# Stage four of a Fourier mixing kernel in quarters of the matmul array, from batch 3

## The chip, the core and the metric

The kernel runs on one core of a Trainium2 chip. The metric is the device time of one execution in microseconds (us). A core has five engines that run side by side and wait for each other by semaphores: TensorE (PE, matrix products), VectorE (DVE), ScalarE (ACT), GpSimd (POOL) and SyncE (SP, which here issues most DMA transfers). Products are written to PSUM, which has eight banks; a bank holds 128 partitions of 512 fp32 numbers.

## What is computed

```python
X = np.fft.rfft(x, axis=1)                    # x: (8, 2496, 256)
Y = X * (filt_r + 1j * filt_i)[None, :, :]
y = np.fft.irfft(Y, n=2496, axis=1).reshape(8 * 2496, 256)
logits = y @ w_gate                           # (19968, 8)
expert = argmax(logits, axis=1)               # gate = its softmax share
for e in range(8):                            # rows sorted by expert
    out[rows of e] = relu(y[rows of e] @ w1[e]) @ w2[e]   # 256 -> 1024 -> 256
out *= gate[:, None]
```

## The kernel before

**The transform.** 2496 = 39 x 64, and the 2496-point transform is done as transforms of 39 and 64 points. For each of the 8 batches there are four stages, each a product with a constant table on PE:

- Stage one (`stage_a`, table `tas`): 39 real points to 20 complex coefficients. Three of the 64 residues stand beside each other on the partitions (3 x 39 = 117 rows in, 3 x 40 = 120 rows out), and 22 *columns* of 256 numbers follow each other. A *chunk* is four columns, the last chunk of a batch two: `CH`. The result goes to DRAM (`zd`).
- Stage two (`stage_b`, `tbs`): 64 points, then DVE multiplies by the filter. Stage three (`stage_c`, `tcs`): 64 points back; the result goes to DRAM (`ud`), one DMA for each four frequencies.
- Stage four (`stage_d`, `tds`): 20 complex coefficients back to 39 real points. A chunk is loaded from `ud` (`load_u`), one product of 512 output columns (120 rows deep, 128 wide) makes two columns of y, and DVE or ACT copies it from its bank into `yo`. The 22nd column holds one residue instead of three, so the last chunk of a batch takes two products of 256, 120 and 40 rows deep.

**Gate and routing.** From `yo` come the logits: for batches 3 to 7 (`by_blocks`) DVE transposes in blocks of 32, and `block_logits` multiplies by the gate weights in four strips of 32 columns of the array. `route` finds the expert and the place of each row, and POOL writes id and gate (eight copies each) behind each row of `yo`, and scatters one column at a time, 117 rows, into the expert's part of `rowsd` (`scatter`), 22 scatters per batch.

**Experts.** As rows of an expert come together, tiles of 512 or 256 rows are read back (`rows_in`), multiplied by w1 and w2 (in part by a scheme with seven block products for eight), scaled by the gate and scattered to the output.

**The order.** All instructions are written in an order that the kernel plans while it is built. The class `Order` keeps an estimated time for each engine and counts a price for each instruction. The main loop, at the end, offers the steps of the transform of slot k (stages two and three of batch k, stage one of batch k+1, stage four of batch k-1) and the two streams of expert products, and takes the first that is ready by the estimate. Each engine then runs its own list strictly in that order. Every call goes through the recording layer, so that the profile shows line 246 for all of them; groups are told apart by the names of their tiles. DMA loads and stores are issued on SP, each in its turn.

Of the kernel before, what the change touches and what calls it, by code (L numbers as in the profile page):

```python
# [34 lines left out]
TK = NB * NS  # L35
DH = D // P
# [4 lines left out]
NJ = D // CT  # L41

# [13 lines left out]
def dft_tables():  # L56
# [24 lines left out]

    ids = np.zeros((NB, N1, NG))
    valid = np.zeros((NB, N1, NG))
    for j in range(NB):
# [3 lines left out]

    by_block = np.zeros((4, CT, NG + 2))
    by_block.reshape(P, NG + 2)[:TP, :NG] = valid.reshape(TP, NG)  # L90
# [5 lines left out]
        "ta": ta.reshape(TP, TK),  # L96
        "tb": tb,
        "tc": tc,
        "td": np.pad(td.reshape(TK, TP), ((0, 0), (0, P - TP))),
        "sg": np.concatenate([sg[:, :NF // 2], sg[:, NF // 2:]]),  # L100
        "ids": ids.reshape(TP, NG),
        "valid": np.concatenate([np.pad(valid.reshape(TP, NG), ((0, P - TP), (0, 0))), by_block], axis=1),
    }


def lay_x(x):

    out = np.zeros((x.shape[0], P, NG, D), x.dtype)
    q = np.arange(N1)
    for j in range(NB):  # L110
        for i in range(len(range(j, N2, NB))):
            out[:, j * N1:(j + 1) * N1, i] = x[:, token(q, NB * i + j)]
    return out
# [11 lines left out]
class Order:  # L125
# [53 lines left out]
    def count(self, engine, op, args, named):  # L179
# [31 lines left out]
        else:  # L211
            if out is None:
                took = 0.8 if engine == "sync" else 0.02
            elif engine == "tensor":
                if start > self.busy + 1.2:
                    self.slow = start + 3.4
                rows = out.ap[0][1]
                took = max(0.1, 0.00085 * n) if op == "transpose" else max(0.216, 0.00169 * n) if rows > 32 else 0.00045 * n
                took *= 2.0 if start < self.slow else 1.0
                tail = 0.25  # L220
            elif engine == "vector":
                took = 0.15 + n / 960
            elif engine == "scalar":
                took = 0.16 + n / 1200
            else:
                took = 0.2 + n / 480
# [24 lines left out]
class Slots:  # L251
# [3 lines left out]
    def freed(self, name, tag):  # L255

        if name is None:
            return 0.0
        if tag in self.live and name in self.live[tag]():
            return 1e9  # L260
        return max(self.order.done.get(name, 0.0), self.order.used.get(name, 0.0)) + 0.1
# [32 lines left out]
def kernel(  # L294
# [12 lines left out]
    ids: bass.AP,  # L307
    valid: bass.AP,
# [25 lines left out]
    TR = E * TE  # L334

    dram = open_pool(ctx, name="dram", bufs=1, space=DRAM)
    zd = [dram.tile([N2, NS, D], F32, tag=f"z{b % 2}", name="zd") for b in range(B)]
    ud = [dram.tile([N2, NS, D], F32, tag=f"u{b % 2}", name="ud") for b in range(B)]


    DR = D + 16
    rowsd = dram.tile([TR, DR], F32, tag="rows", name="rows")
# [17 lines left out]
    tas = cst.tile([TP, TK], F32, name="tas")  # L360
    tbs = cst.tile([P, P], F32, name="tbs")
    tcs = cst.tile([P, P], F32, name="tcs")
    tds = cst.tile([TK, P], F32, name="tds")
# [15 lines left out]
    ids0 = cst.tile([TP, NG], F32, name="ids0")  # L379
    vld = cst.tile([P, 2 * NG + 2], F32, name="vld")  # L380
# [12 lines left out]
    ps.live["bank"] = lambda: ()  # L393
# [25 lines left out]
    def load_filters(c):  # L419
        f0, n = FH[c]  # L420
        if c == 0:
            nc.sync.dma_start(out=tbs, in_=tb)
# [11 lines left out]
        if c == 0:  # L434
            nc.sync.dma_start(out=tcs, in_=tcm)

    def load_rest():
        nc.sync.dma_start(out=tds, in_=td)
# [33 lines left out]
    def columns(ap, i0, n):  # L472

        rows = ap.rearrange("t s d -> (t s) d")
        m = min(n, NG - 1 - i0)
        yield TK, slice(0, m), rows[i0 * TK:(i0 + m) * TK, :].rearrange("(i p) d -> p i d", p=TK)
        if m < n:
            yield NS, slice(m, n), rows[(NG - 1) * TK:, :].rearrange("(i p) d -> p i d", p=NS)
# [23 lines left out]
    def by_part(ap):  # L502

        return ap.rearrange("t (c f) d -> (t c) f d", c=2)

# [8 lines left out]
    def load_z(b, c):  # L514
        f0, n = FH[c]
        zi = fin(("z", b, c))
        nc.sync.dma_start(out=zi[:, :n], in_=by_part(zd[b])[:, f0:f0 + n, :])

    def load_u(b, c):
        i0, n = CH[c]  # L520
        ui = fin(("u", b, c))
        for r, m, v in columns(ud[b], i0, n):
# [5 lines left out]

    def stage_a(b, c):
        i0, n = CH[c]  # L530
        xt = ins.pop(("x", b, c))
        zo = sb.tile([TK, 4, D], F32, tag="st", name="zo", bufs=4)
        for j in range(0, n, 2):
            p = bank()
            mm(p[:TK, :], lhsT=tas, rhs=xt[:TP, j:j + 2, :], start=True, stop=True)
            evac(zo[:, j:j + 2, :], p[:TK, :].rearrange("p (t d) -> p t d", t=2), 512)
        for r, m, v in columns(zd[b], i0, n):
# [4 lines left out]
    def stage_b(b, f):  # L542
# [6 lines left out]
        mm(p, lhsT=tbs, rhs=zi[:, j:j + 2, :], start=True, stop=True)  # L549
# [13 lines left out]

    def stage_c(b, f):
# [6 lines left out]
        mm(p, lhsT=tcs, rhs=ys, start=True, stop=True)  # L571
        evac(uo[:, j:j + 2, :], p.rearrange("p (i d) -> p i d", i=2), 512)
        if j == 2:
            f0 = f - 2
            move(by_part(ud[b])[:, f0:f0 + 4, :], uo)
# [3 lines left out]
    def stage_d(b, c):  # L579
# [7 lines left out]
        yo = outs["o", b, c] = sb.tile([P, 4, DR], F32, tag="y", name="yo", bufs=YB)  # L587
        for j in range(0, n, 2):
            p = bank()
            if i0 + j + 2 < NG:  # L590
                mm(p, lhsT=tds, rhs=ui[:TK, j:j + 2, :], start=True, stop=True)
# [6 lines left out]


# [12 lines left out]
    def first_a(c):  # L612
        i0, n = CH[c]
        xt = ins.pop(("x", 0, c))
        for j in range(0, n, 2):
            p = bank()[:, :4 * TK]
            for h in range(DH):
                for i in range(2):
                    mm(p[:, (2 * h + i) * TK:(2 * h + i + 1) * TK], lhsT=xt[:TP, j + i, h * P:(h + 1) * P], rhs=tas,
# [21 lines left out]
    def first_c(f):  # L641
        ys = outs.pop(("y", 0, f))
        p = bank().rearrange("p (h i t c) -> p h i t c", h=DH, c=2, i=2)
        for i in range(2):
            for h in range(DH):
                mm(p[:, h, i].rearrange("p t c -> p (t c)"), lhsT=ys[:, i, h * P:(h + 1) * P],
                   rhs=tcs, start=True, stop=True)
# [90 lines left out]
    def route(b, c0, c1):  # L738
# [63 lines left out]
        if by_blocks(b):  # L802
# [13 lines left out]
            nc.vector.tensor_copy(row.rearrange("p (c g) -> p g c", g=4), pr[:, :, 0])  # L816
# [5 lines left out]
        for i, yo in enumerate(yos):  # L822
            n = min(4, w - 4 * i)
            sh8 = (TP, n, 8)
            nc.gpsimd.tensor_scalar(
                yo.bitcast(I32)[:TP, :n, D:D + 8], in0=ids0[:, t0 + 4 * i:t0 + 4 * i + n, None].to_broadcast(sh8),
# [3 lines left out]
        for i in range(w):  # L830
            m = N1 if t0 + i == NG - 1 else TP
            rows.append((row[:m, i:i + 1], yos[i // 4][:m, i % 4, :]))
        for i, (at, what) in enumerate(rows):
            m = what.ap[0][1]
            nc.gpsimd.tensor_copy(what[:, D + 8:], sd[:m, i:i + 1].to_broadcast((m, 8)))
# [7 lines left out]
    def pad_rows():  # L843
# [7 lines left out]
        nc.gpsimd.memset(fill.bitcast(I32)[:, D:D + 8], N)  # L851
# [96 lines left out]
    def rows_in(i):  # L948
# [4 lines left out]
        ng = gis[i] = pools["moe"].tile([P, 4, DR - D], F32, tag="ng", name="ng", bufs=8)  # L953
# [128 lines left out]
    def result(i, j):  # L1082
# [12 lines left out]
        gate = gis[i][:, j, 8:9]  # L1095
# [49 lines left out]
    def result_by_quarters(i):  # L1145
# [7 lines left out]
        gate = gis[i][:, :, 8:9]  # L1153
# [62 lines left out]
    def slot(k):  # L1216
# [12 lines left out]
        elif k < B:  # L1229
            for f in range(0, NF + 4, 2):  # L1230
                at = f / (NF + 4)
                if f < NF:
                    steps.append((at, lambda f=f: stage_b(k, f), ("z", k, f // 4) if f % 4 == 0 else None, 0.85, "b", lambda f=f: count("y") < 4 and [ins["z", k, f // 4]]))
                if f >= 4:
                    steps.append((at + 0.01, lambda f=f: stage_c(k, f - 4), None, 0.85, "c", lambda f=f: [outs["y", k, f - 4], 0.0 if f % 4 else sb.free("st") - 0.9]))
        if k + 1 < B:
            for c in range(nch):
                steps.append(((0.25 if k == 0 else 0.0) + 0.7 * c / nch, lambda c=c: stage_a(k + 1, c), ("x", k + 1, c), 0.43 * CH[c][1], "a", lambda c=c: [ins["x", k + 1, c], sb.free("st") - 0.9]))
        if k > 0:
            for c in range(nch + 3):  # L1240
# [3 lines left out]
                if c < nch:  # L1244
                    steps.append((at, lambda c=c: stage_d(k - 1, c), ("u", k - 1, c) if k > 1 else "y", 0.43 * CH[c][1], "d",
                                  lambda c=c: [ins["u", k - 1, c] if k > 1 else outs["ui", c], sb.free("y") - 0.9]))
                if by_blocks(k - 1):
                    if 1 <= c <= nch:
                        steps.append((at + 0.03, lambda c=c: turn_y(k - 1, c - 1), None, 0.0, "d", lambda c=c: len(yts) < 2 and [outs["o", k - 1, c - 1]]))
# [174 lines left out]
    def second_products():  # L1424

        for i in range(NT - RARE):
            if late and i < LARGE:
# [37 lines left out]
    with tc.manual_schedule(engines=None):  # L1465
        warm()
        nc.sync.dma_start(out=tas, in_=ta)
# [5 lines left out]
        def wait_of(f):  # L1473
# [11 lines left out]
            banks = ps.free("bank") if f[3] < 0.9 else max(ps.free("bank"), ps.free("bank", 1) - 0.85)  # L1485
# [15 lines left out]
        while fs or any(heads):  # L1501
# [7 lines left out]
            choice[0 if credit > 0.0 or not fs else 1:0] = products  # L1509
# [64 lines left out]
```

## Time and profile before

| | |
|---|---|
| median of 3 runs | 1470.89 us (1468.29 to 1471.23) |
| the profiled execution | 1474.5 us, its span 1472.8 us |
| mean granted PE clock | 0.992 |
| PE products of stage four, 512 columns, from DRAM | x140 records, 606 ns mean, 67.4 us busy |
| row scatters on POOL | x176, 1034 ns mean |
| result scatters on POOL (128 rows) | x161, 1003 ns mean |
| y copies, ACT and DVE | x82 of 588 ns, x6 of 681 ns |
| DMA | 278.19 MB, mean 189 GB/s |

A group of the profile is written as line, engine, operation, output tile <- input tiles, shapes, count, then busy time in us and the mean in ns. The records of PE overlap: a record's length covers also the time that its data takes through the array, so the pace is read from the starts. One fp32 product stands as two MATMUL records. The shape `120*128` in a PE row is rows times columns of the array in use. "PEld" are weight loads. In the page's 40 slices PE has 8 or 9 tenths in nearly all of them, and DMA is above 8 tenths in most of the first nine.

### The profile page before, as it was taken

Reading aid. Unit: us, or ns where it says so; the run is one execution under the profiler, and the core shown is the slowest. Engines: PE = TensorE matmul, PEld = TensorE weight load, DVE = VectorE, ACT = ScalarE, POOL = GpSimd, SP = SyncE. Lnnn points to the kernel's source line nnn. Section 1 sums busy time; section 2 is a strip of 40 time slices with the busy share of each in tenths; the row PEclk is TensorE's granted clock in tenths of the full one; section 3 lists DMA queues with packets and bytes.
Section 4 is the critical chain, followed back from the end, with each engine's and each line's share of the span. In section 5 each row is a group of like instructions: output and inputs, shape, how many; then the busy total and the mean of one; then the engine's idle time right before and its main releaser. Section 6 shows DMA issues by size and latency. Waiting matters only on the chain.

```text
span 1472.8 us, 25703 instructions
## 1 busy us (share of the span) xinstructions
PE 1438.4 (98%) x7828; PEld 1148.5 (78%) x7828; DVE 835.8 (57%) x1818; ACT 480.5 (33%) x1005; POOL 818.9 (56%) x1214
## 2 busy tenths in 40 slices
PE   8998999999999999999999999999999999999998
PEld 5553555777577777777787778889999999999997
DVE  4666568335766574566757554566878775531110
ACT  3553443233232333222223232222232322223332
POOL 3434355525456654565375567647989878831111
PEclk9999999999999999999999999999999999999999
DMA  9749798887786576557345644548665424456661
GB/s 255 243 156 339 250 323 257 271 260 222 246 246 189 169 253 180 150 167 251 105 126 151 205 117 132 149 128 244 175 186 154 133 77 139 135 191 176 173 192 42
DMA packets 216383, 278.19 MB, mean 189 GB/s; under 512 B 124131, under 2 KB 163708, under 8 KB 216245
## 3 DMA queue, kind: packets, MB, share of 16 engines
q1 hardware_dynamic: 197125, 233.19, 53.7%
q0 software_dynamic: 19120, 43.33, 8.5%
q8 instruction: 66, 1.08, 0.3%
q14 instruction: 72, 0.59, 0.1%
HBM read 196.45 MB, written 80.64 MB: 188 GB/s over the span
## 4 chain that ended last, share of the span: by engine, by line
PE 85%; DMA 6%; DVE 4%; issue 2%; POOL 1%; SPq 1%; ACT 1%; POOLq 0%; DVEq 0%; ACTq 0%
PE bank L246 85%; DMA fin<-in_x_dram 2%; DMA fin<-ud 2%; DVE yw L246 1%; DVE ys L246 1%; DMA ud<-uo 1%; DMA fin<-zd 1%; SPq L246 1%; POOL out_dram L246 0%; DVE hT L246 0%; DMA w1t<-in_moe_w_dram 0%; DMA ng<-rows 0%; ACT hT L246 0%; DMA zd<-zo 0%; DMA xg<-rows 0%
## 5 line engine op out<-in xcount | busy, mean ns | idle before, releaser
L246 DVE TENSOR_TENSOR hT<-bank,hT 128x512 f32<-128x512 f32 (+1 forms) x504 | 300.8, 626 | 165.4 <-PE bank L246 77.7
L246 PE MATMUL bank<-w2t,hT 128*128 128x256 f32 (+1 forms) x1984 | 387.5, 350 | 2.4 <-DVE hT L246 1.4
L246 PEld LDWEIGHTS bank<-w2t,hT 128*128 128x128 f32 x1984 | 335.1, 190 | 53.0 <-issue 11.7
L246 PE MATMUL bank<-xT,w1t 128*128 128x256 f32 (+1 forms) x1728 | 316.3, 329 | 0.2 <-DVE hT L246 0.2
L246 POOL DMA_INDIRECT out_dram<-ys,ng x161 | 161.5, 1003 | 271.6 <-ACT ys L246 136.7
L246 PEld LDWEIGHTS bank<-xT,w1t 128*128 128x128 f32 x1728 | 265.4, 192 | 32.4 <-issue 8.3
L246 ACT ACTIVATE hT<-hT 128x1024 f32<-128x1024 f32 (+1 forms) x144 | 135.0, 959 | 390.5 <-DVE hT L246 387.5
L246 POOL DMA_INDIRECT rows<-yo,row x176 | 181.9, 1034 | 74.8 <-POOL yo L246 38.5
L246 ACT ACTIVATE ys<-bank,ng 128x256 f32<-128x256 f32 x104 | 49.3, 474 | 303.9 <-PE bank L246 235.2
L246 PE MATMUL bank<-sums,wsum 128*128 128x256 f32 (+1 forms) x576 | 135.6, 358 | 0.0
L246 PE MATMUL bank<-w2s,hT 128*128 x592 | 132.6, 379 | 0.0
L246 PEld LDWEIGHTS bank<-w2s,hT 128*128 128x128 f32 x592 | 110.3, 190 | 13.8
L246 PEld LDWEIGHTS bank<-sums,wsum 128*128 128x128 f32 x576 | 100.5, 190 | 17.7 <-issue 6.8
L246 POOL TENSOR_TENSOR wsum<-w1t 128x256 f32<-128x256 f32 x72 | 56.5, 785 | 82.2 <-PE bank L246 57.7
L246 DVE STREAM_TRANSPOSE xT<-xg 128x512 f32<-128x512 f32 (+2 forms) x126 | 57.4, 493 | 54.6 <-PE bank L246 51.4
L246 DVE TENSOR_TENSOR ys<-bank,ht 128x512 f32<-128x512 f32 x80 | 54.8, 685 | 52.2 <-PE bank L246 42.9
L246 PE MATMUL bank<-fin,tas 117*120 117x512 f32 x154 | 77.3, 622 | 6.9 <-DMA fin<-in_x_dram 6.7
L246 PE MATMUL bank<-fin,tds 120*128 120x512 f32 (+1 forms) x168 | 76.1, 573 | 3.9 <-DMA fin<-ud 3.3
L246 PE MATMUL bank<-fin,tbs 128*128 128x512 f32 x140 | 72.6, 605 | 5.4 <-DMA fin<-zd 5.4
L246 PE MATMUL bank<-ys,tcs 128*128 128x512 f32 x140 | 73.3, 611 | 4.2 <-DVE yw L246 3.4
L246 ACT ACTIVATE hT<-bank 128x128 f32<-128x128 f32 (+1 forms) x191 | 57.6, 303 | 52.5 <-PE bank L246 42.9
L246 PE MATMUL bank<-xT,wsum 128*128 128x256 f32 (+1 forms) x288 | 67.8, 358 | 0.2 <-ACT yo L246 0.2
(171 smaller groups left out, 1766.6 us busy)
## 6 DMA issues: line engine op xcount, KB each, us to landing
w1t<-in_moe_w_dram SPq DMA_DIRECT2D x126, 512.0 KB
w2t<-in_moe_w_dram SPq DMA_DIRECT2D x68, 512.0 KB
fin<-in_x_dram SPq DMA_DIRECT2D x39, 512.0 KB
fin<-zd SPq DMA_DIRECT2D x35, 512.0 KB
ud<-uo SPq DMA_DIRECT2D x35, 512.0 KB
fin<-ud SPq DMA_DIRECT2D x35, 512.0 KB
zd<-zo SPq DMA_DIRECT2D x35, 480.0 KB
xg<-rows SPq DMA_DIRECT2D x112, 128.0 KB
```

What stands on the lines that cost most here:

```text
L246: return real(*args, **named)
```

## The change

It has these parts:

1. **Quarters.** From batch 3 (`BD = 3`) the rows of a column are laid out so that the 60 real parts lie on partitions 0 to 59 and the 60 imaginary ones on 64 to 123; partitions 60 to 63 and 124 to 127 are pads. A chunk's four products each use 60 rows and 64 columns of the array, with 512 output columns (256 in a last chunk): one product for each pair of (real or imaginary rows) and (first or second half of the chunk's columns). Real rows give the even half of the 39 points, imaginary rows the odd half, each in a bank of its own. The odd half is copied to `yo`, then `fold_y` makes even + odd and even - odd by two DVE instructions that read the even half in its bank.
2. **Tiles of u apart.** Batches 3 to 7 write u into two DRAM tensors of their own (`halves_apart`). A store of stage three becomes two, of 126 and of 2 partitions (`by_part`). `fill_between` writes the pads and the last column once, with filter values, in slot 1: four DMAs.
3. **Row scatters of 128 rows.** The rows of a column in the new layout fill all 128 partitions. Rows that stand for no token get places behind the experts' parts (320 for each batch, `lids`), chosen by a maximum when the row numbers are made. `DR` falls from 272 to 264: id and gate are written four times instead of eight.
4. **Tables** are loaded into [128, 128] tiles, each a second time later on (`load_table`). The same layout is written for stages one and two from batch `BA = 8`, which no batch reaches.
5. **The planner** gets prices for products of 64 rows out, a rule for the bank that a fold still needs, changed rules for free banks and for the order of choices, and one rule for the start of the last expert products. The tile for ids and gates (`ng`) has 7 buffers instead of 8.

```diff
+BA, BD = 8, 3
...
+                if op == "matmul" and rows == 64 and n > D // 2:
+                    took = 0.29 if n > D else 0.17
...
-    ud = [dram.tile([N2, NS, D], F32, tag=f"u{b % 2}", name="ud") for b in range(B)]
+    ud = [dram.tile([NG * P, D], F32, tag=f"u{b % 2}", name="ud") for b in range(BD)]
+    halves_apart = [dram.tile([NG * P, D], F32, tag=f"v{b}", name="ud") for b in range(2)]
+    ud[BD:] = [halves_apart[b % 2] for b in range(B - BD)]
...
-    DR = D + 16
-    rowsd = dram.tile([TR, DR], F32, tag="rows", name="rows")
+    DR = D + 8
+    rowsd = dram.tile([TR + NW * B, DR], F32, tag="rows", name="rows")
...
-    ps.live["bank"] = lambda: ()
+    ps.live["bank"] = lambda: {p.name for key, p in outs.items() if key[0] == "odd"}
...
+    def fill_between():
+        for u in halves_apart:
+            at = u[TH, :]
+            nc.sync.dma_start(out=bass.AP(at.tensor, at.offset, [[64 * D, 2 * NG - 2], [1, 4 * D]]), in_=ht[:2 * NG - 2, :4, :].rearrange("p f d -> p (f d)"))
+            nc.sync.dma_start(out=u[(NG - 1) * P:, :], in_=ht[:, 0, :])
...
-            move(by_part(ud[b])[:, f0:f0 + 4, :], uo)
+            for of, v in by_part(ud[b], uo, b >= BD, f0, 4):
+                move(v, of)
...
+        if b >= BD:
+            m = n // 2
+            both = [bank() for _ in range(2)]
+            for h in range(2):
+                for part in range(2):
+                    k = slice(64 * part, 64 * part + TH)
+                    mm(both[part][64 * h:64 * h + 64, :m * D].rearrange("p (i d) -> p i d", i=m), lhsT=tds[k, :64],
+                       rhs=ui[k, h * m:(h + 1) * m, :], start=True, stop=True)
+            evac(yo[:, m:n, :D], both[1][:, :m * D].rearrange("p (i d) -> p i d", i=m), m * D)
+            outs["odd", b, c] = both[0]
+            return
...
+    def fold_y(b, c):
+        m = CH[c][1] // 2
+        even = outs.pop(("odd", b, c))[:, :m * D].rearrange("p (i d) -> p i d", i=m)
+        yo = outs["o", b, c]
+        nc.vector.tensor_tensor(yo[:, :m, :D], even, yo[:, m:2 * m, :D], op=ALU.add)
+        nc.vector.tensor_tensor(yo[:, m:2 * m, :D], even, yo[:, m:2 * m, :D], op=ALU.subtract)
...
-            nc.vector.tensor_copy(row.rearrange("p (c g) -> p g c", g=4), pr[:, :, 0])
+            nc.vector.scalar_tensor_tensor(
+                out=row.rearrange("p (c g) -> p g c", g=4),
+                in0=lids[:, NG + t0:NG + t0 + wide].rearrange("p (c g) -> p g c", g=4), scalar=float(b * NW),
+                in1=pr[:, :, 0], op0=ALU.add, op1=ALU.max)
...
-        ng = gis[i] = pools["moe"].tile([P, 4, DR - D], F32, tag="ng", name="ng", bufs=8)
+        ng = gis[i] = pools["moe"].tile([P, 4, DR - D], F32, tag="ng", name="ng", bufs=7)
...
-            if late and i < LARGE:
+            if late and i < LARGE and (wide or i in made):
...
-            banks = ps.free("bank") if f[3] < 0.9 else max(ps.free("bank"), ps.free("bank", 1) - 0.85)
+            banks = 0.0 if not f[3] else ps.free("bank") if f[3] < 0.9 and f[4] not in "ad" else max(ps.free("bank"), ps.free("bank", 1) - 0.85)
...
-            choice[0 if credit > 0.0 or not fs else 1:0] = products
+            head = next((n for n, c in enumerate(choice) if c[0][4] not in ("x", "y")), 0) + 1
+            choice[0 if credit > 0.0 or not fs else head:0] = products
```

## The prediction

> **What bounds the kernel now.** I read the page's first two parts, then the busy time by stretches of the span, then the timeline of TensorE (PE) around the changed products.
>
> ```profile
> span 1472.8 us, 25703 instructions
> PE 1438.4 (98%) x7828; PEld 1148.5 (78%) x7828; DVE 835.8 (57%) x1818; ACT 480.5 (33%) x1005; POOL 818.9 (56%) x1214
> ...
> PE 85%; DMA 6%; DVE 4%; issue 2%; POOL 1%; SPq 1%; ACT 1%; POOLq 0%; DVEq 0%; ACTq 0%
> ```
>
> PE is busy for 98% of the span and holds 85% of the chain that ended last; no other engine passes 57%. A busy PE is a modelled thing, so I asked where its gaps lie. Columns of the next view: stretch, its length, then busy time and count for PE, its weight loads, DVE, ACT, POOL; granted clock, DMA share, GB/s.
>
> ```profile
> 100.00:200.00 100.00, 90.99 (x327) 48.54 (x327) 64.06 (x159) 42.12 (x94) 44.44 (x74) 0.95 0.90 303
> ...
> 390.00:520.00 130.00, 128.61 (x616) 93.57 (x615) 88.47 (x185) 40.89 (x80) 72.27 (x113) 1.00 0.73 222
> 520.00:680.00 160.00, 160.00 (x778) 122.59 (x777) 104.80 (x218) 50.22 (x96) 89.91 (x141) 1.00 0.62 184
> 680.00:820.00 140.00, 139.21 (x696) 110.47 (x695) 85.75 (x182) 40.39 (x76) 82.64 (x128) 1.00 0.55 162
> ```
>
> PE's gaps are early (9 us lost in 100 to 200). The products of stage four that change belong to batches 3 to 7 and run between 287 and 880 us; there PE is full at a granted clock of 1.00, DVE at 55 to 68%. Time taken from PE's work there is time taken from the span, as long as nothing else falls behind.
>
> **What the changed products cost now.** A 512-column product stands in the trace as two MATMUL records.
>
> ```profile
> 691.39 1.88 PE L246 MATMUL bank<-fin,tds 120*128 120x512 f32 x4
> 693.11 1.03 PE L246 MATMUL bank<-sums,wsum 128*128 128x256 f32 x4
> ```
>
> A full chunk (four columns) is two products, four records, 693.11 - 691.39 = **1.72 us**, so 0.43 a record. The last chunk of a batch (two columns) has two products of 256, the second over 40 rows only:
>
> ```profile
> 451.88 1.22 PE L246 MATMUL bank<-fin,tds 120*128 120x256 f32 x4
> 453.03 1.12 PE L246 MATMUL bank<-fin,tbs 128*128 128x512 f32 x2
> 453.99 1.02 PE L246 MATMUL bank<-ys,tcs 128*128 128x512 f32 x2
> ```
>
> It takes 1.15 us, and the two records behind it take 0.96 instead of 0.86: **1.25 us** together, where four records of 256 columns are worth 0.86. The missing 0.39 is the price of going to a part of the array's rows and back.
>
> **What they will cost.** The changed kernel has four products per chunk, each of 60 rows and 64 columns of the array in a quarter of its own, two records each. No row of before has quarters. The nearest is the gate's product over 32-column strips, four strips side by side:
>
> ```profile
> 642.01 1.03 PE L246 MATMUL bank<-xT,wsum 128*128 128x256 f32 x4
> 642.97 0.64 PE L246 MATMUL bank<-yt,wb 128*32 128x128 f32 x16
> 643.54 0.92 PE L246 MATMUL bank<-w2t,hT 128*128 128x256 f32 x3
> ```
>
> A 256-column record takes 0.216 us (half of 0.43). The four records before end their pace at 642.01 + 4 x 0.216 = 642.87; the work behind starts at 643.54, and its first record takes 0.32 instead of 0.216 (0.92 for three, less 0.38 for the last one's length, is two paces of 0.54). So 16 records of 128 columns, worth 16 x 0.107 = 1.71 us one after another, cost 643.54 - 642.87 + 0.10 = 0.77. Four at a time they are worth 0.43; the remaining 0.34 is the price of the excursion. Strips side by side really run side by side here.
>
> Here a rule speaks against the change. The Trainium skill (TensorE: Matmul & The Clock Gate, "What overlaps and what doesn't") says that a weight load overlaps running products only if its row group differs, and that products keep strict order. In program order the two records of one quarter follow one another, so by the rule they couldn't share the array with the next pair: first record alone, then second with the neighbour's first, and so on, five record times, 5 x 0.43 + 0.36 = 2.51 us a chunk, **20 us slower** in all. But the strips above all use the same 128 rows, also have two records each, and ran four abreast. I take the row. What the row can't show is two row halves working at once. The skill (TensorEngine Tiling (Array Packing), "Key Properties") has tiles operate independently, and the first page ("Measured speedup vs the span model") measures packing of rows and columns together at 6.3 times for nine tiles, 0.7 of the ideal; 0.7 of four would be 1.72 x 2 / 2.8 = 1.23 us a chunk, an estimate.
>
> My sum from the rows: a full chunk is two record times and one excursion, 0.86 + 0.365 (between 0.34 and 0.39) = 1.225, saving 0.495. 25 such chunks: 12.4 us. The last chunk: 2 x 0.216 + 0.365 = 0.80 for 1.25, saving 0.45, five times: 2.3. In the built order two quarter chunks stand back to back once, which saves one excursion, 0.37. PE's other products are the same in kind and number. **PE loses 15 us of work**; bounds 14 to 16.5 if quarters run abreast.
>
> **The other parts.**
> - *Folds.* Each chunk had two evacuations and now has one plus two DVE adds out of a bank. A DVE add of this shape (ys from bank and ht, 128x512) takes 685 ns, of 256 columns 420: 50 x 0.685 + 10 x 0.42 = 38.5 us more DVE, against some 29 copies fewer on ACT (588 ns each, 17 us). DVE goes from 62% to about 69% between 287 and 880. Behind a fold in DVE's queue stand the adds of hT, which free the banks for the next expert products. Their waits are small today: PE waits 2.0 us for DVE hT in the whole run. Bounds: nothing (a negative value I exclude, as DVE only gets work), and the whole 38.5 if every fold held up PE. The crowded places are 380 to 420 and 440 to 460 us, where DVE is 17 of 20 busy. I take 1.5, near the present wait.
> - *Bank held.* The even half stays in its bank till the fold: one bank of eight for about a microsecond. In the 1.5.
> - *Row scatters of 128 rows.* A scatter of 117 rows costs POOL 1034 ns and one of 128 rows (the results) 1003, so rows don't set the price: 0. The count stays 176. Bytes grow by 320 waste rows x 5 batches x 1056 = 1.7 MB and shrink by 32 in each of some 20,000 rows; DMA is 45 to 73% busy there. POOL writes four copies of id and gate instead of eight: a shade less than 219 ns each.
> - *Pads written once.* Four more transfers, 0.6 MB, near 65 us, from a table that has long landed. Between 40 and 100 us the same view shows 181 GB/s at 57% DMA: 3.3 us of transfer; the loads of stage-one results queue behind them on SP. Bounds 0 and 3; I take 0.5.
> - *More issues on SP.* 25 stores of two partitions, five table loads and one of ids, five u loads fewer: some 26 issues of 0.35 us, 9 us over 600. SP's queue spends 462 us waiting for PE, so this hides. The reloads of the four tables also wait for PE's last use of the old one, and stand before stores of u and weight loads; PE is by then one step away. 0 to 1 us; I take 0. The reloads for stages one and two serve no product, as their batch limit lies past the last batch.
> - *One buffer fewer for ids and gates* (7 for 8), the planner's changed prices and rules: a different mixture of the same products. In the built order PE's work is the same up to the first expert products (247 us). Either sign, 2 us; I take 0.
>
> Sum: -15 + 1.5 + 0.5 = **-13 us**. Against the profiled execution, a span of 1472.8 (1474.5 in all), that is a span near 1460. The runs' median, 1470.9, lies 3.6 below that execution; 1470.9 - 13 = **1458**.
>
> **Rivals.**
> 1. *The row halves take turns* (slower). If two quarters that differ in rows don't run together, a full chunk is four record times: 4 x 0.43 + 0.365 = 2.085, 0.365 worse; last chunks stay equal. 25 x 0.365 = 9, with the 2 of losses **1482**; by the rule above 20 + 2, 1493. It decides from 3.1 record times per chunk upwards, where my sum has 2. For it: no row of before shows two row parts at once, and the 40-row product ran alone. Against: strips of columns run fully abreast, and the halves write different banks.
> 2. *DVE becomes the bound at the crowded places.* If each of the 30 folds delays the hT adds so that PE waits 0.2 to 0.3 us, 6 to 9 us return: **1464 to 1467**. For it: 17 of 20 at 380 to 420. Against: 5 to 10 of 20 in many other places, and eight banks.
> 3. *It doesn't reach the span.* The gain is real, but the new order loses it early, where DMA decides (pads in front of the first loads, stores in two pieces): **1470**, no change. Against: PE's order there is the same, and PE is full in every stretch where time is saved.
>
> **How the numbers follow.** Forecast -13 us: 0.70, own range 1451 to 1464. Rival 2: 0.11. Rival 3: 0.07. Rival 1: 0.12. What can be told from no change is 0.2%, 2.9 us: faster means under 1468. Faster 0.70 + 0.11 = 0.81; same 0.07; slower 0.12. For the range I take the forecast and rival 2, 1451 to 1469; outside are rival 1 and most of rival 3.
>
> **What would show it.** Quarter chunks in the timeline: eight records whose next neighbour starts about 1.1 to 1.25 us after the first; starts of four records together. At 2.1 or more, rival 1. PE's waits for DVE hT: under 4 us; above 8, rival 2. PE busy falls by about 15 us, DVE rises by 38, the count of scatters stays 176 at about 1.03 us. The early stretch, up to 287 us, lasts as long as now. I am wrong if PE's full stretches gain idle slices, or if an excursion into quarters costs much more than 0.39.

## The result and the profile after

| | before | after |
|---|---|---|
| median | 1469.55 us, 10 runs (1467.28 to 1472.07) | 1463.43 us, 10 runs (1461.57 to 1469.55) |
| ratio | 1 | 0.9961 [0.9948, 0.9973] |
| profiled execution | 1474.5 us, span 1472.8 us | 1469.55 us, span 1467.8 us |

The change takes 6.1 us off the median, 0.4%, where 13 were forecast; the forecast's range, 1451 to 1469, holds the result. The profiled execution before lies above its ten runs, the one after is the slowest of its ten. They differ by 5.0 us, near the difference of the medians, so the two traces may be set side by side.

The first two parts of the page of the changed kernel, the chain of waits, and the scatters' group:

```profile
span 1467.8 us, 26013 instructions
PE 1424.7 (97%) x7948; PEld 1132.3 (77%) x7948; DVE 871.3 (59%) x1881; ACT 462.0 (31%) x977; POOL 812.6 (55%) x1215
...
PE 84%; DMA 7%; issue 4%; DVE 3%; POOL 2%; ACT 1%; SPq 1%; POOLq 0%; DVEq 0%; ACTq 0%
...
L296 POOL DMA_INDIRECT rows<-yo,row x176 | 180.5, 1026 | 71.1 <-POOL yo L296 30.5
```

PE is busy 13.7 us less and DVE 35.5 us more, about as forecast; ACT loses 18.5. The span falls by 5.0 only, so PE stands idle 8.7 us longer than before. The timeline of PE shows a full chunk in quarters and a last chunk (start, length, records):

```profile
288.25 1.67 PE L296 MATMUL bank<-xT,w1t 128*128 128x256 f32 x7
289.85 1.09 PE L296 MATMUL bank<-fin,td 60*64 60x512 f32 x8
290.87 0.40 PE L296 MATMUL bank<-oe,tri 117*117 117x48 f32 x2
```

```profile
344.20 1.10 PE L296 MATMUL bank<-ys,tc 128*128 128x512 f32 x2
345.23 0.66 PE L296 MATMUL bank<-fin,td 60*64 60x256 f32 x8
345.83 0.70 PE L296 MATMUL bank<-xT,w1t 128*128 128x256 f32 x2
```

Eight records of 512 columns take 290.87 - 289.85 = 1.02 us from their first start to the neighbour's. With 0.09 lost on the way in and 0.10 by the first record behind them, both read from the starts of single records, a full chunk costs 1.22 us. The single records of the trace also show the four quarters at once: four records start within 0.02 us, the other four 0.48 us later. A last chunk takes 0.60 to its neighbour and, with the same two losses, 0.79.

Where the idle time is, the busy times by stretches tell. Columns as in the prediction: stretch, length, PE, weight loads, DVE, ACT, POOL, granted clock, DMA share, GB/s. Here is the stretch in which nearly all changed chunks lie, of the kernel before, and then of the changed one:

```profile
300.00:880.00 580.00, 576.45 (x2870) 435.74 (x2868) 358.94 (x761) 179.62 (x358) 321.53 (x502) 1.00 0.63 188
```

```profile
300.00:880.00 580.00, 571.58 (x3020) 427.40 (x3021) 397.45 (x857) 166.31 (x337) 328.04 (x523) 1.00 0.65 195
```

PE's idle time is the length less its busy time: 3.55 us before, 8.42 after. The stretch that was full has got holes, 4.9 us of them (another 3.5 us come up to 300 us), while DVE went from 62% (358.94 of 580) to 69%. The folds stand in the groups of DVE, by form:

```profile
L296 DVE TENSOR_TENSOR yo<-bank,yo 128x512 f32<-128x512 f32 x50 | 34.2, 686 | 2.1 <-ACT yo L296 1.0
L296 DVE TENSOR_TENSOR yo<-bank,yo 128x256 f32<-128x256 f32 x10 | 4.2, 421 | 0.5 <-ACT yo L296 0.3
```

That is 38.4 us, as priced (38.5). Yet the list of what PE waited for does not name them (total us, times, longest):

```profile
PE bank L296 <- DMA fin<-in_x_dram: 8.8, 3, 4.1
PE bank L296 <- issue: 5.8, 4, 4.2
PE bank L296 <- DMA fin<-ud: 3.7, 2, 2.3
...
PE bank L296 <- DVE ys L296: 3.1, 3, 1.5
PE bank L296 <- ACT ls L296: 1.8, 1, 1.8
PE bank L296 <- DVE yw L296: 1.8, 1, 1.8
PE bank L296 <- DVE hT L296: 1.8, 3, 0.7
PE bank L296 <- POOL w2t L296: 1.5, 1, 1.5
```

PE waits 1.8 us for DVE's hT, where it waited 2.0 before. By the sign that the prediction set (above 8) the folds cost nothing. New or longer are waits of one to three times each: for DVE's ys, for ACT's ls, for POOL's w2t and wsum. And one hole stands apart, in front of the first chunk in quarters:

```profile
258.55 1.95 PE L296 MATMUL bank<-fin,ta 117*120 117x512 f32 x4
264.66 1.98 PE L296 MATMUL bank<-fin,td 60*64 60x512 f32 x8 [4.16 <-issue]
266.58 5.64 PE L296 MATMUL bank<-w2t,hT 128*128 128x256 f32 x16
```

PE stands for 4.16 us, and then runs slowly: those eight records take 1.92 us instead of 1.02.

So three causes were to be told apart. **F**: the folds hold DVE, and through it PE. **U**: the new reads and writes of u, above all the second piece of each store, come late for the first chunk in quarters. **O**: another planned order happens to be a little worse.

### The profile page after: what moved, and what is told of

Read it like the earlier page. It is cut to its first block, busy times and chain, and to the rows that moved or that the text cites. A ratio compares the mean times of both kernels' runs of the same rounds, so it can differ in the third digit from the quotient of the medians.

```text
span 1467.8 us, 26013 instructions
## 1 busy us (share of the span) xinstructions
PE 1424.7 (97%) x7948; PEld 1132.3 (77%) x7948; DVE 871.3 (59%) x1881; ACT 462.0 (31%) x977; POOL 812.6 (55%) x1215
## 4 chain that ended last, share of the span: by engine, by line
PE 84%; DMA 7%; issue 4%; DVE 3%; POOL 2%; ACT 1%; SPq 1%; POOLq 0%; DVEq 0%; ACTq 0%
PE bank L296 84%; DMA fin<-in_x_dram 2%; DMA fin<-zd 1%; DMA fin<-ud 1%; DVE hT L296 1%; DMA rows<-yo,row 1%; DMA w1t<-in_moe_w_dram 1%; POOL out_dram L296 1%; POOL rows L296 1%; SPq L296 1%; DMA ud<-uo 0%; DVE yw L296 0%; POOL wsum L296 0%; DMA zd<-zo 0%; DVE ys L296 0%
## 5 line engine op out<-in xcount | busy, mean ns | idle before, releaser
L296 POOL DMA_INDIRECT rows<-yo,row x176 | 180.5, 1026 | 71.1 <-POOL yo L296 30.5
L296 ACT ACTIVATE ys<-bank,ng 128x256 f32<-128x256 f32 x96 | 45.5, 474 | 285.0 <-PE bank L296 228.0
L296 PE MATMUL bank<-fin,ta 117*120 117x512 f32 x154 | 76.3, 615 | 8.1 <-DMA fin<-in_x_dram 7.9
L296 PE MATMUL bank<-fin,tb 128*128 128x512 f32 x140 | 74.4, 621 | 4.0 <-DMA fin<-zd 3.4
L296 PE MATMUL bank<-ys,tc 128*128 128x512 f32 x140 | 72.9, 607 | 3.1 <-DVE ys L296 3.1
L296 PE MATMUL bank<-sums,w1t 128*128 128x256 f32 (+1 forms) x288 | 67.2, 356 | 0.0
```

Of the source, the lines that this page charges most:

```text
L296: return real(*args, **named)
```

## The experiments

The ratios are to the kernel before, measured beside each of three groups of experiments: 1467.27 us (12 runs) beside the changed kernel again, no folds, one store piece and no quarters; 1469.03 (29) beside folds doubled, the other order of the kernel before, the later stage four and the fold on POOL; 1469.01 (31) beside the rest. A ratio, with its 95% interval, is worked out from all runs and need not be that of the two medians; where the two differ by more than a microsecond, both are told.

### The changed kernel again

No edit; the base for the folds taken away, the store in two pieces, and all of the change but the quarters.

> The changed kernel as it is. Three theories for the 7 us that the forecast had too much: F (the DVE folds make PE wait at crowded places), U (the loads of u for the first quarter chunk, at 260 us, wait for the stores of u, which now come in two pieces; PE waits 4.2 us and then runs some 4 us at half clock, 6 us in all), O (the new planned order is worse by itself). All: 1461 to 1465 us. F: PE gaps between 300 and 880 us add up to 7 us or more again (8.4 in the first profile, 3.6 in the kernel before). U: a gap over 3 us in front of the first quarter product again. O: gaps of this size lie elsewhere, at places that change from run to run.

1460.70 us, ratio 0.9949 [0.9930, 0.9969]: 6.6 us below the kernel before. PE's idle time between 300 and 880 us is 5.65 us in this execution, under the 7 that F expected; the hole in front of the first chunk in quarters is there again, 4.76 us.

### The folds taken away

```diff
-        nc.vector.tensor_tensor(yo[:, :m, :D], even, yo[:, m:2 * m, :D], op=ALU.add)
-        nc.vector.tensor_tensor(yo[:, m:2 * m, :D], even, yo[:, m:2 * m, :D], op=ALU.subtract)
+        for o in (yo[:, :m, :D], yo[:, m:2 * m, :D]):
+            nc.count("vector", "tensor_tensor", (o, even, yo[:, m:2 * m, :D]), {})
+        nc.nc.scalar.copy(out=yo[:, :m, :D], in_=even)
```

The planner still counts both adds, so the order stays the changed kernel's. DVE's work goes, and ACT gets 30 copies, 16 us, that also free the bank of the even half. y is wrong in this kernel, so rows may go to other experts; the instructions stay the same in number.

> The two DVE folds of each chunk are replaced by one ACT copy of the even half, in the same planned order, so the even and odd halves are not combined. DVE loses 38 us, ACT gains 17. F: PE gaps between 300 and 880 us fall under 4.5 us, and the time is 4 to 6 us below the changed kernel, 1457 to 1460. U and O: within 1.5 us of the changed kernel.

1453.93 us, ratio 0.9909 [0.9887, 0.9930]: 6.8 us below the changed kernel beside it, more than the 4 to 6 expected, and 13.3 below the kernel before. The six runs lie between 1452.51 and 1459.26 us, the seven of the changed kernel between 1456.58 and 1463.27. F holds in kind; how much of the 6.8 the folds themselves make is read from the traces below. The stretch from 300 to 880 us:

```profile
300.00:880.00 580.00, 576.60 (x3058) 435.05 (x3057) 367.15 (x794) 178.14 (x366) 330.71 (x528) 1.00 0.64 193
```

Idle time of PE: 3.40 us, as before the change. DVE is down to 63%.

### The folds doubled

```diff
+        for _ in range(2):
+            nc.nc.vector.tensor_tensor(yo[:, :m, :D], even, yo[:, m:2 * m, :D], op=ALU.subtract)
```

> Two more DVE adds of the fold's kind behind each first fold (50 of 685 ns and 10 of 420, 38 us of DVE), in the same planned order; the last one rewrites a result that is there already, so the even-plus-odd rows hold the difference. F: as much again as the removal gave or more, 6 to 10 us slower than the changed kernel, 1467 to 1471, and the gaps of PE between 800 and 1010 us grow. O (the place of the products in the order decides, not DVE): within 2 us of the changed kernel.

1468.26 us, ratio 1.0000 [0.9988, 1.0012]. The whole gain is gone: by the two ratios of the changed kernel, 0.9961 and 0.9949, another 38 us of DVE work costs 5.7 to 7.5 us. The size is as F expected. (Here too y is wrong.)

```profile
300.00:880.00 580.00, 569.75 (x2996) 426.43 (x2995) 432.48 (x910) 164.05 (x333) 322.52 (x514) 0.99 0.63 193
```

PE's idle time is 10.25 us. No folds, folds, folds twice: 3.4, 5.65 to 8.4, 10.25 us idle; 1453.9, 1460.7, about 1467 us on the base of the first group. The medians rise with the work, by about 0.17 us for each us that DVE gets; the intervals are too wide to say whether evenly. The gaps of PE between 800 and 1010 us, which F expected to grow, did not: 3.9 us, after 4.6 and 3.7 in the changed kernel's two executions.

### The same work on DVE in the kernel before

```diff
+            if b >= 3:
+                nc.nc.vector.tensor_tensor(yo[:, j:j + 2, :D], p.rearrange("p (i d) -> p i d", i=2), yo[:, j:j + 2, :D], op=ALU.max)
```

It stands behind each copy of y from batch 3, is not counted by the planner, and leaves y as it is. No quarters, no new order.

> The kernel before, in its own order, with one more DVE instruction behind each copy of y from batch 3 on: the maximum of the bank and the copy, which changes nothing in the result. 55 instructions of 512 columns, 38 us of DVE, as the folds. F: DVE work of this size at this place costs PE time also without quarters: 4 to 8 us slower than the kernel before. O: within 2 us.

1472.63 us, ratio 1.0034 [1.0016, 1.0053]: 5.0 us more by the ratio, 3.6 by the medians. F holds again. DVE's group, by form:

```profile
L598 DVE TENSOR_TENSOR yo<-bank,yo 128x512 f32<-128x512 f32 x55 | 37.1, 688 | 31.8 <-ACT yo L246 29.2 <-DMA out_dram<-ys,ng 1.0
```

And the stretch:

```profile
300.00:880.00 580.00, 572.94 (x2841) 433.13 (x2840) 390.50 (x814) 178.28 (x354) 322.08 (x507) 1.00 0.61 186
```

For 37.1 us of DVE work PE is idle 7.06 us in the stretch, where it was 3.55. So work of this kind has its price without quarters and without a new order. The added instruction reads the bank behind the copy, as a fold does, so a bank held longer is not told apart from DVE's time by this. One wait of PE is for such a bank:

```profile
PE bank L246 <- DVE yo L598: 1.0, 1, 1.0
```

No wait of this kind stands in the lists of the changed kernel's two executions.

### How a fold reaches PE

No folds, folds and folds twice have the same order, so the time from one chunk in quarters to the next can be compared. Here are the first and the last chunk without folds, with folds (the changed kernel's second profiled run), and with folds twice:

```profile
256.92 1.66 PE L296 MATMUL bank<-fin,td 60*64 60x512 f32 x8 [2.52 <-DVE zo L296]
842.88 0.66 PE L296 MATMUL bank<-fin,td 60*64 60x256 f32 x8
```

```profile
259.70 1.98 PE L296 MATMUL bank<-fin,td 60*64 60x512 f32 x8 [4.76 <-issue]
848.54 0.66 PE L296 MATMUL bank<-fin,td 60*64 60x256 f32 x8
```

```profile
262.48 1.09 PE L296 MATMUL bank<-fin,td 60*64 60x512 f32 x8 [3.60 <-issue]
860.23 0.66 PE L296 MATMUL bank<-fin,td 60*64 60x256 f32 x8
```

The 30 chunks, two of them back to back, bound 28 stretches. From start to start, in us:

| | no folds | folds | folds twice |
|---|---|---|---|
| first to last chunk | 585.96 | 588.84 | 597.75 |
| the stretch near 400 to 440 us | 34.81 | 35.34 | 39.64 |
| the stretch near 820 to 840 us | 17.75 | 19.55 | 21.92 |
| first to second chunk | 24.02 | 24.57 | 24.06 |
| the other 25 together | 509.38 | 509.38 | 512.13 |

In 25 of the 28 stretches the folds cost nothing, to a hundredth of a microsecond on the whole. The cost lies at two places, 0.5 and 1.8 us in this pair. (The 0.55 of the first stretch begin with its first chunk, 1.98 us for 1.66, in front of every fold.) In the run without the second store pieces, below, which has the same order and all folds, the two stretches take 34.37 and 21.06 us: only the second place is sure for the folds. From first to last chunk the folds cost 2.9 us here, 2.7 in that run, and 5.1 in the first profiled execution (591.02 us), where 2.2 of them lie in two stretches with a wait for "issue". As many folds again cost 8.9 us, most of it at both places. In the kernel before, 37 us of added DVE work lengthen the same way from 589.15 to 592.10 us, by 2.95, of which 2.0 fall in one stretch at 404 to 416 us and 0.8 in one at 434 to 443.

That is less than the 6.8 us between the medians. The two executions shown differ by 5.8 us: 2.8 are there when the first chunk starts, in front of every fold, 2.9 lie between first and last chunk, and 0.1 behind. The 2.8 are not the folds' work.

A place where the changed kernel (its second profiled run) waits, and the one without folds does not; the order of both is the same. First DVE in the changed kernel, then PE:

```profile
819.46 1.42 DVE L296 TENSOR_TENSOR yo<-bank,yo 128x512 f32<-128x512 f32 x2
820.79 0.17 DVE L296 TENSOR_TENSOR past<-tau,end 1x35 f32<-1x35 f32 x1
...
822.29 0.59 DVE L296 TENSOR_SCALAR take<-take 1x8 f32<-1x8 f32 x1
...
823.11 0.58 DVE L296 TENSOR_SCALAR take<-take 1x8 f32<-1x8 f32 x1
823.73 0.64 DVE L296 TENSOR_TENSOR done<-done,take 1x8 f32<-1x8 f32 x1
824.30 1.87 DVE L296 TENSOR_TENSOR hT<-bank,hT 128x512 f32<-128x512 f32 x3
```

```profile
821.88 1.89 PE L296 MATMUL bank<-xT,w1t 128*128 128x256 f32 x8
825.72 1.10 PE L296 MATMUL bank<-sums,wsum 128*128 128x256 f32 x4 [1.95 <-DVE hT L296]
```

Then the same in the kernel without folds, DVE and PE:

```profile
817.12 0.16 DVE L296 TENSOR_SCALAR take<-take 1x8 f32<-1x8 f32 x1
...
817.51 0.16 DVE L296 TENSOR_SCALAR take<-take 1x8 f32<-1x8 f32 x1
817.70 0.15 DVE L296 TENSOR_TENSOR done<-done,take 1x8 f32<-1x8 f32 x1
817.78 1.87 DVE L296 TENSOR_TENSOR hT<-bank,hT 128x512 f32<-128x512 f32 x3
```

```profile
818.02 1.89 PE L296 MATMUL bank<-xT,w1t 128*128 128x256 f32 x8
819.75 1.03 PE L296 MATMUL bank<-sums,wsum 128*128 128x256 f32 x4
```

DVE runs its list in order. Between a fold and the three adds of hT, which free banks, stands a chain of a dozen small instructions (the map of the expert tiles). Without folds the adds begin 818.02 - 817.78 = 0.24 us *before* the eight products that run meanwhile, and PE never waits. With the fold they begin 824.30 - 821.88 = 2.42 us *behind* the same products, 2.66 us later against PE. The fold's own share is 820.79 - 819.46 = 1.33 us, from its start to that of the next instruction. Three small instructions take 0.58 to 0.64 us here and 0.15 to 0.16 there, another 1.3 us. In the changed kernel they fall together with POOL's adds for wsum; in the other kernel those start at 818.27, when the chain is through.

```profile
822.13 0.73 POOL L296 TENSOR_TENSOR wsum<-w1t 128x256 f32<-128x256 f32 x1 [2.59 <-PE bank L296]
822.94 0.73 POOL L296 TENSOR_TENSOR wsum<-wsum,w1t 128x256 f32<-128x256 f32 x1
823.63 0.72 POOL L296 TENSOR_TENSOR w1t<-w1t 128x256 f32<-128x256 f32 x1
```


1.95 us of the lateness reach PE. This is the second place of the table. The waits for ACT's ls and DVE's ys in the list above are not the folds' work: they stand in front of the first fold (ls at 228 us; 2.4 us also without folds). The one for POOL's w2t, at 1011 us, stands behind the last.

### The store in two pieces

```diff
-                move(v, of)
+                if b >= BD and of.ap[0][1] == 2:
+                    moves.append((of, lambda of=of, v=v: nc.count("sync", "dma_start", (), {"out": v, "in_": of})))
+                else:
+                    move(v, of)
```

> The store of two partitions that follows each store of u is left out, in the same planned order, so the last column keeps its filler. U: if the second piece is what comes late, the gap in front of the first quarter product falls from 4 to under 2 us and the time by 3 to 5 us, to 1458 to 1461. F and O: within 1 us of the changed kernel.

1459.89 us, ratio 0.9936 [0.9915, 0.9957], against 1460.70 for the changed kernel: no difference that these runs can tell. The hole in front of the first chunk in quarters is still there, 6.02 us. U falls, as far as the second pieces are meant.

### All of the change but the quarters

```diff
-BA, BD = 8, 3
+BA, BD = 8, 8
...
-            nc.vector.scalar_tensor_tensor(
-                out=row.rearrange("p (c g) -> p g c", g=4),
...
+            nc.vector.tensor_copy(row.rearrange("p (c g) -> p g c", g=4), pr[:, :, 0])
```

> The changed kernel with its limit for stage four at batch 8: no quarters, no folds, scatters of 117 rows, whole stores of u; what stays are the planner's rules, the narrower rows, 7 buffers for ids, the table reloads and the filling of the pads. O: 4 to 8 us slower than the kernel before, 1474 to 1478. F and U: within 3 us of the kernel before, 1467 to 1473.

1480.05 us, ratio 1.0080 [1.0060, 1.0100]: 12.8 us *above* the kernel before by the medians, 11.7 by the ratio, more than any of the three expected. Its timeline of PE has one large hole:

```profile
252.87 2.19 PE L296 MATMUL bank<-fin,ta 117*120 117x512 f32 x4
263.65 3.75 PE L296 MATMUL bank<-fin,td 120*128 120x512 f32 x4 [8.58 <-DMA fin<-ud]
```

8.58 us, and the four records behind it take 3.55 us, where they took 1.72. Either the rest of the change costs 13 us, and the quarters win back 19, or this order is an accident. A change of one price of the planner tells, as it moves all choices a little:

```diff
-    HOP = 0.1
+    HOP = 0.11
```

> The changed kernel without quarters (limit for stage four at batch 8), with the planner's step between engines priced 0.11 for 0.10, which gives another order. If the 13 us that the version without quarters lost are an accident of its order (8.6 us of waiting and a half clock at 255 us), this one lies within 4 us of the kernel before and has no gap over 5 us there. If the rest of the change (narrow rows, 7 buffers, reloads, pads) costs by itself, it is again 9 us or more slower than the kernel before.

1473.75 us, ratio 1.0024 [1.0005, 1.0043]: 3.5 us above the kernel before by the ratio, 4.7 by the medians, and the longest hole near 255 us is 4.22 us. Some 8 us were an accident of order. What remains, 3.5 us (0.7 to 6.3), is one order's cost of the rest of the change, and can't be told from another accident.

### Other orders of the two kernels

The same edit in the kernel before and in the changed one.

> The kernel before with one price of the planner moved by a hundredth of a microsecond (the step between engines counts 0.11 for 0.10): the same instructions, in another order from the 380th product on. O: the order alone moves the time by 4 us or more either way. F: within 3 us of the kernel before.

> The changed kernel with the planner's step between engines priced 0.11 for 0.10: the same instructions, in another order from the 380th product on. F: 4 to 9 us below the kernel before, as the changed kernel. O: the order decides, and it lies more than 4 us from the changed kernel, on either side.

Before: 1470.07 us, ratio 1.0006 [0.9992, 1.0019], though the order of its products differs from the 380th on. After: 1461.98 us, ratio 0.9950 [0.9928, 0.9972]. In the other pair of orders the gain is 7 to 8 us, in the first 6 to 7: much the same, as F expected. What both orders share, O can't explain by this.

### Stage four of batch 3 later

In the changed kernel the planner puts the first chunk in quarters at 264.7 us, where the first of batch 3 before came at 287.0. This edit puts batch 3's stage four later in its slot:

```diff
-                at = ... (0.35 if k == 2 else 0.2) + 0.8 * c / (nch + 3)
+                at = ... (0.35 if k in (2, 4) else 0.2) + 0.8 * c / (nch + 3)
```

> The changed kernel with stage four of batch 3 offered later in its slot (from 0.35 of it, not from 0.2). U: the gap of 4 to 5 us in front of the first quarter product and the half clock behind it go, 3 to 6 us less than the changed kernel, 1455 to 1458. F: within 2 us, as the folds stay. O: any difference up to 5 us, with gaps at other places.

1459.28 us, ratio 0.9938 [0.9919, 0.9958]: 1.4 us below the changed kernel's 1460.70, which is within F's 2 us and short of the 3 to 6 of U. The hole in front of the first quarters is gone, but others grow: between 200 and 300 us PE is idle 8.2 us in all, after 8.3 in the changed kernel. That hole was one of several of a stretch in which DMA is 86% busy (before: 6.1 us idle), and moving a step moves it elsewhere.

### Half of the fold on POOL

```diff
-            evac(yo[:, m:n, :D], ..., m * D)
+            either(odd, m * D, lambda: nc.vector.tensor_scalar(..., scalar1=2.0, ...),
+                   lambda: nc.scalar.activation(yo[:, m:n, :D], odd, AF.Copy, scale=2.0))
...
-        nc.vector.tensor_tensor(yo[:, :m, :D], even, yo[:, m:2 * m, :D], op=ALU.add)
-        nc.vector.tensor_tensor(yo[:, m:2 * m, :D], even, yo[:, m:2 * m, :D], op=ALU.subtract)
+        nc.vector.scalar_tensor_tensor(out=yo[:, :m, :D], in0=yo[:, m:2 * m, :D], scalar=0.5, in1=even, op0=ALU.mult, op1=ALU.add)
+        nc.gpsimd.tensor_tensor(yo[:, m:2 * m, :D], yo[:, :m, :D], yo[:, m:2 * m, :D], op=ALU.subtract)
```

The copy keeps 2 x odd; DVE makes even + odd in one instruction, and POOL subtracts 2 x odd from it.

> The odd half is copied doubled; DVE makes even plus odd with half of it, and POOL takes the doubled odd half off that for even minus odd: 19 us of DVE go, POOL gains some 35 us. F: 2 to 4 us less than the changed kernel, 1457 to 1459. U and O: no sign that follows from DVE, within 3 us either way, by the order.

1459.22 us, ratio 0.9937 [0.9919, 0.9955]: 9.8 us below the kernel before. PE's idle time between 300 and 880 us is 4.5 us. DVE loses half of its folds, POOL gets 35.5 us (25 of 1278 ns, 5 of 728). The planner counts these instructions, so this is a new order as well, and the 1.5 us against 1460.70 are under what F expected and can't be put down to DVE. Together with the later stage four:

> Half the fold on POOL and stage four of batch 3 later in its slot, together. F and U: the two gains add up, 10 to 13 us below the kernel before. O: no sum, as the order is a new one: anything from 5 to 12 below.

1466.95 us, ratio 0.9986 [0.9972, 1.0001]. The gains don't add; they vanish. In this order PE waits for DVE as in no other:

```profile
PE bank L296 <- DVE hT L296: 8.8, 9, 2.2
```

The planner makes its own order of these two edits, and why DVE comes late in it nine times was not settled. It misses every expectation, and it limits what the two single runs say: their intervals overlap that of the changed kernel (0.9948 to 0.9973 in its first runs), so each beats the kernel before for certain and the changed kernel only perhaps. They have the lowest medians of the kernels here that compute the whole result.

## Why the prediction was right and where it was wrong

**Quarters on PE: right.** A full chunk was put at 1.225 us and takes 1.22; a last one at 0.80, takes 0.79; the excursion, read from the strips of 32 columns, was worth 0.365 and is 1.22 - 0.86 = 0.36. So the saving of 15 us of PE work stands, and the kernel without folds agrees with it in the total: 13.3 us below before (10 to 17 by its interval), where the sum without its 1.5 for folds says 14.5. The row halves don't take turns (rival 1). Choosing the row against the skill's rule was right: as the prediction read that rule, a chunk would have cost 2.5 us.

**Reaching the span: right in the main, with a loss in the early stretch that was put at nothing but the pads' 0.5.** With folds away the gain arrives, so rival 3, that all of it is lost early, falls. But the stretch from 200 to 300 us, most of it in front of the first fold, got worse. Before, and then after:

```profile
200.00:300.00 100.00, 93.94 (x402) 63.92 (x401) 63.86 (x194) 37.35 (x85) 55.05 (x93) 0.98 0.86 275
200.00:300.00 100.00, 91.66 (x409) 60.72 (x409) 61.33 (x171) 33.66 (x80) 50.09 (x85) 0.95 0.86 257
```

PE is idle 8.3 us for 6.1, and the granted clock falls from 0.98 to 0.95, which is worth another 3 us (an estimate: 3% of 100 us). In the other executions of this order PE is idle 7.6 and 10.1 us at a clock of 0.95, 9.4 at 0.98 (folds twice) and 6.4 at 0.97 (no folds). Together that is 1 to 7 us more than before. It is too unsteady to be priced from single executions, and no experiment takes it away by itself; but it is of the size of what the folds leave unexplained.

**Folds: here the prediction failed.** Its words: "Their waits are small today: PE waits 2.0 us for DVE hT in the whole run", and "I take 1.5, near the present wait". Taking the folds away gives 6.8 us by the medians, doubling them costs 5.7 to 7.5, the same work in the kernel before costs 3.6 to 5.0; between first and last chunk the traces show 2.7 to 5.1 for the folds. With 6.8 the sum is -15 + 0.5 + 6.8 = -7.7, where -6.1 to -7.0 were measured; with 3 to 5 it is -11.5 to -9.5, and the early stretch has to give the rest. Which share is whose stays open.

The step that failed is the reading of a present wait as the price of more work. The present wait is the sum over places where DVE is late *now*; it says nothing of the places that come within a microsecond or two of being late, and a fold moves those. The range of 0 to 38.5 was open on purpose, but the value was taken near one end, from one row.

Rival 2 had the right engine, with 0.11, and a total of 1464 to 1467 near the one measured. Its mechanism was not quite what happened: not every fold delays PE by 0.2 to 0.3 us, two places take most. One, 400 to 440 us, overlaps those that the prediction calls crowded (380 to 420 and 440 to 460). The other is not one of them: in the kernel before, DVE is busy 11.5 of 20 us from 820 to 840. And the fullest, 660 to 680 us with 18.3 of 20, which the prediction did not name, cost nothing when work was added there (51.49 and 51.48 us from chunk to chunk, without and with). The chain of waits was a better guide than the busy share: in the kernel before, between 287 and 880 us, it runs over DVE at three places only, 383 to 405, 695 to 703 and 840 us, and two of them are near where the cost came.

**The sign set for rival 2 was wrong as well.** Waits for hT were 1.8 us in the first execution and 3.7 in the second, under the mark of 4, while the cost was there. The sign that did show is the last one of the prediction: PE's full stretches gained idle time, 3.55 to 8.4 and 5.65 us. Idle time alone still misses a part, as PE counts as busy at a lower clock too: with folds twice, the hole of 3.66 us at 836.75 is followed by 5.25 us at a mean clock of 0.67.

**Other parts.** Scatters of 128 rows: right, x176 at 1026 ns for 1034. Second store pieces: 0 fits, as the medians with and without them differ by 0.8 us and their runs overlap. The other issues on SP were not tried alone. Bank held: not tried alone, as every experiment that moves DVE's work moves the time of a bank too; no wait of PE for a fold's bank is listed in the changed kernel. Pads: not tried.

**Planned order: the size was wrong for the general case.** "Either sign, 2 us" holds between the two orders of the kernel before (+1) and of the changed one. It doesn't hold for two others: one order cost 8 us against its neighbour (no quarters), and two edits that each gained a little, not clear of noise, together lost 4 to 5 us against the changed kernel.

## What to carry to other kernels

Work that is added to an engine with time to spare is not free when that engine runs in order and frees the bottleneck's banks. Its price can't be read from the wait that stands in the trace today, nor from the engine's busy share, but at the places where the bottleneck has little ahead of that engine (here 0.08 to 0.18 us of span for each us of DVE work, by trace or by medians). To test such a price, add the work to the kernel before, without the rest of the change; doubling it in the changed kernel gives a second point. Where the order stays the same, compare the time from mark to mark of the two traces: it tells at which places the cost lies, and what of a difference stands in front of the edit and can't be its work. Where a program plans its own order, measure a second order (one price changed by a tenth) before a result of a few microseconds is put down to an edit.

## What the runs showed of the hardware that was not expected

- Lateness on DVE can feed itself. Three small instructions of 0.15 to 0.16 us took 0.58 to 0.64 when they ran beside POOL's adds for wsum: each ended with the add (at 822.88, 823.69 and 824.37 us, the adds at 822.86, 823.67 and 824.35), and one at 822.91, between two adds, took 0.16. A delay of 1.3 us, which pushed them there, became 2.66. This was seen at one place.
- The price of DVE work is not spread: 38 us of it left 25 of 28 stretches as long as they were, and cost PE 2.3 us at two others. Another 38 us cost 8.9 and reached more places.
- After some holes PE works at half its pace, and a hole then costs more than its own length: eight records of 512 in quarters took 1.92 us instead of 1.02 at 264.66, at a granted clock of 0.50, and four plain ones 3.55 instead of 1.72 after the hole of 8.58 us. Not at once after each: behind a hole of 3.60 us (folds twice, 262.48) the eight took 1.02 us, and the products behind them were slow.
